# Decay attention and two gated MLPs in one kernel: a tile's attention cut into two halves of 64 tokens

## The chip, the cores and the metric

The kernel runs on one core of a Trainium2 chip. The metric is device time in microseconds (us), as the median of a few executions; a profile of one further execution gives the trace that the rows below are read from. TensorE does the matrix products (PE in the rows, its weight loads PEld), VectorE (DVE), ScalarE (ACT) and GpSimd (POOL) work element by element, and SyncE (SP) issues the transfers.

## What is computed

Inputs are `r, k, v` of 4 batches, 8 heads, 768 tokens and 48 dimensions, a decay `w` and a bonus `u`. The attention is a recurrence with one 48x48 state per head:

```python
for t in range(S):
    kt, vt, rt = (k[:, :, t], v[:, :, t], r[:, :, t])
    cur = np.einsum('bhd,bhe->bhde', u[None] * kt, vt)
    y[:, :, t] = np.einsum('bhd,bhde->bhe', rt, state + cur)
    state = w[None, :, :, None] * state + np.einsum('bhd,bhe->bhde', kt, vt)
```

Its output, 3072 tokens by 384, goes through two gated MLPs with 1536 hidden units. The first normalises its input and uses `g * sigmoid(g) * val`, the second `sigmoid(g) * val`; each multiplies by its output weights. Weights arrive in double precision, and a product in the MLPs is made of three single-pass products of high and low parts.

## The kernel before

**Tiles and blocks.** The tokens are 24 attention tiles of 128; tile i is chunk i // 4 of batch i % 4, so that a batch's state is needed again four tiles later. Four tiles make a block of 512 tokens, and there are six blocks. Each MLP layer handles a block in 12 steps, one for each 128 hidden units; a step is nine matmuls for the gate (lines 678 to 680), nine for the value, and nine or twelve for the output (line 705), all 512 or 384 columns long. Attention of later blocks is put between the steps of earlier ones. The first five tiles run before the first step.

**One tile's attention.** The decay is folded into `kq` and `rq` ahead of the products. Their transposes `kT` and `rT` hold a pair of heads in rows 0 to 47 and 64 to 111, so that the two heads of a pair lie in the two row halves of the array.
1. *Scores* (line 498): for each of four pairs and both heads, `kT` of 48x128 stays in the array and 128 columns of `rT` stream through, into one bank per head of the pair.
2. *Update* (line 502): `kq` transposed times `v` over all 128 tokens, eight products of 48x48, into a third bank. The last chunk of a batch has none.
3. VectorE multiplies the scores by a 128x128 triangular mask into `aa` (line 512), two instructions of 512 columns.
4. *Result*: the old state `z` enters with 32 products (line 525; none in the first chunk), each with 32 tokens as the array's columns; then `aa` times `v` with 32 products (line 530), over all 128 rows of the array and again with 32 tokens as columns.
5. VectorE adds the bonus term `vc` (line 536) and makes the new state `(z + update) * wc` (lines 545, 548 and 466), `wc` being the decay of a whole tile, which `state_factors` prepares at the start (line 417).

Each of these fp32 products shows in the trace as two MATMUL records.

**What sets the order.** `Plan` holds tasks with an engine, a price in us, a due time and the buffers that they read and write. `run` issues them in the order that its own clock finds, engine by engine, and hands out the eight PSUM banks. `DUE` gives the due time of a tile's attention against its block's first step, `LEAD` that of a weight piece's steps, `STEP` how far the elementwise part of an MLP step is preferred, and `S_US` and `Y_US` are the prices of the score task (scores and update) and of the result task. Each engine then works through its list strictly in order. Weights of the first layer come in as 36 pieces: a load, two ScalarE passes (lines 64 and 71), two VectorE ones (lines 80 and 81), a GpSimd sum (line 87), and high and low parts (lines 640 and 643).

Of the kernel before, what the change touches and what calls it, by code (L numbers as in the profile page):

```python
# [7 lines left out]
F32 = mybir.dt.float32  # L8
# [4 lines left out]
ALU = mybir.AluOpType  # L13
AX = mybir.AxisListType

P = 128
HS = 112
NPAIR = 4
# [6 lines left out]
DUE = (-75, 4), (-36, 5), (-41, 6)  # L25


LEAD = 17, 20, 18, 15, 14, 18
STEP = 12


Y_US, S_US = (1.4, 0.95), (1.6, 1.1)
# [198 lines left out]
def blocked(  # L231
# [31 lines left out]
    def ring(name, n, shape, dtype=F32):  # L263
        return [work.tile(shape, dtype, name=f"{name}{i}") for i in range(n)]
# [8 lines left out]
    mask = const.tile([P, P], F32, name="mask")  # L273
# [15 lines left out]
    x, z = ring("x", 2, [P, DM]), ring("z", B, [HS, NPAIR, D])  # L289
    xh, xl = ring("xh", 2, [P, KC, N], F32R), ring("xl", 2, [P, KC, N], F32R)  # L290
# [12 lines left out]

    half_of = lambda a, n: a.rearrange("p (q a) d -> p a q d", a=2)[:, n]
# [23 lines left out]
    def setup():  # L328
# [3 lines left out]
        def warm(banks):  # L332
            for bank in banks:
                nc.tensor.matmul(plan.banks[bank][:, :NPAIR * D], o[0][:, :P], o[0][:, :NPAIR * D], start=True, stop=True)
# [7 lines left out]
        for t in (kn[0], rn[0], kq[1], rq[0]):  # L342
# [11 lines left out]
        nc.gpsimd.affine_select(out=mask, in_=mask, compare_op=ALU.is_gt, fill=0.0,  # L354
                                base=0, pattern=[[1, P]], channel_multiplier=-1)
# [101 lines left out]
    def attention(i):  # L457
# [37 lines left out]
        def scores(*sp):  # L495
            for p in range(NPAIR):
                for n in range(2):
                    nc.tensor.matmul(sp[n][:, p * P:(p + 1) * P], kT[i2][rows(n), p, :], rT[i2][rows(n), p, :], start=True, stop=True)  # L498

        def update(up):  # L500
            for h in range(H):
                nc.tensor.matmul(up[rows(h % 2), h // 2 * D:(h // 2 + 1) * D], kq_[:, h, :], vn[i3][:, h, :], start=True, stop=True)  # L502

        def both(*ps):
            scores(*ps[:2])
            if not last:
                update(ps[2])
        more = [] if last else [name("up")]
        add("T", S_US[last], d + 3, both, [(t, i2, n) for t in ("kT", "rT") for n in range(2)] + ([] if last else [("kq", i2), ("v", i3)]),
            [name("sp")] + more, psum=[name(("sp", n)) for n in range(2)] + more, gate=[("aa", n) for n in range(2)])  # L510
        for n in range(2):
            add("V", 0.6, d + 3 + n, lambda sp, n=n: nc.vector.tensor_tensor(  # L512
                out=aa[0][:, n], in0=sp.rearrange("p (q t) -> p q t", q=NPAIR),
                in1=mask.unsqueeze(1).to_broadcast([P, NPAIR, P]), op=ALU.mult),
                [name("sp")], [("aa", n)], psum=[name(("sp", n))])
# [3 lines left out]
        quarters = [slice(t, t + P // 4) for t in range(0, P, P // 4)]  # L519
# [12 lines left out]
        banks = [name(("yp", n)) for n in range(2)]  # L532
        add("T", Y_US[first], d + 6, result, [("aa", 0), ("aa", 1), ("v", i3)] + ([] if first else [("rT", i2, 0), ("rT", i2, 1), ("z", b)]),
            [name("yp")], psum=banks, gate=[("x", i2)])
# [5 lines left out]


        if not last:
            u3 = lambda up: up[:HS, :NPAIR * D].rearrange("p (q e) -> p q e", q=NPAIR)
            if first:
                add("V", 0.27, d + 9, lambda up: nc.vector.tensor_tensor(out=z[b], in0=u3(up), in1=wc, op=ALU.mult),
                    [name("up"), "wc"], [("z", b)], psum=[name("up")])
            else:
                add("V", 0.27, d + 9, lambda up: nc.vector.tensor_tensor(out=z[b], in0=u3(up), in1=z[b], op=ALU.add),
                    [name("up")], [("z", b)], psum=[name("up")])
                add("VG", (0.27, 0.6), d + 9, either(z[b], z[b], wc, ALU.mult), ["wc"], [("z", b)])  # L550


        t = ss[i2]
# [212 lines left out]
    plan.add("V", 1.0, DUE[0][0] + 4, state_factors, (), ["wc", ("sg", 1)])  # L766
    plan.add("V", 0.3, DUE[0][0] + 16, start_ok, (), ["ok"])
# [189 lines left out]
```

## Time and profile before

| | us |
|---|---|
| median of three runs | 1038.29 (1037.9 to 1042.92) |
| the profiled execution | 1038.28 |
| its span, first to last instruction | 1036.6 |
| TensorE busy | 1013.8 (98%) |
| VectorE busy | 494.6 (48%) |
| ScalarE busy | 342.0 (33%) |
| GpSimd busy | 140.5 (14%) |

The profiled execution is as long as the median run, and 1.7 us of it lie outside its span. A matmul's recorded duration overlaps that of the next, since they are pipelined; what a matmul costs TensorE is the time from its start to the start of the next. Busy shares are averages over the whole span: the first 140 us, in which weights are prepared, look different from the rest.

### The profile page before, as it was taken

How to read it: one execution, taken by the hardware profiler on the slowest of the kernel's cores; microseconds unless marked ns; L12 is line 12 of the kernel's file. 1: busy time of each engine (PE TensorE's matmuls, PEld its weight loads, DVE VectorE, ACT ScalarE, POOL GpSimd, SP SyncE). 2: the span in 40 equal slices, each digit the busy share in tenths (PEclk: the TensorE clock that was granted, in tenths of full speed). 3: DMA queues.
4: the chain of work that ended last, by engine and by line, in shares of the span. 5: the costliest groups of instructions: out<-in, count | busy, mean ns of one | idle time of the engine just before them, and what ended most of it. 6: DMA issues, size and time to landing. Idle time of an engine off the chain costs nothing.

```text
span 1036.6 us, 18973 instructions
## 1 busy us (share of the span) xinstructions
PE 1013.8 (98%) x7746; PEld 841.5 (81%) x7746; DVE 494.6 (48%) x967; ACT 342.0 (33%) x710; POOL 140.5 (14%) x167
## 2 busy tenths in 40 slices
PE   7898999999999999999999999999999999999997
PEld 6686777787787777878888888888888888888886
DVE  8989975746654764563456322322222222222222
ACT  4676542223333333333455412222212212212121
POOL 4534342201212321111011000000000000000000
PEclk7999999999999999999999999999999999999999
DMA  9924446645783775553655200100100100000000
GB/s 191 265 88 123 116 84 134 113 92 138 155 199 85 166 177 127 135 147 116 183 157 175 73 1 1 61 1 1 61 1 20 42 1 1 31 1 21 11 1 34
DMA packets 213759, 91.37 MB, mean 88 GB/s; under 512 B 156576, under 2 KB 205984, under 8 KB 213664
## 3 DMA queue, kind: packets, MB, share of 16 engines
q1 hardware_dynamic: 213664, 90.08, 35.1%
q8 instruction: 62, 1.02, 0.4%
q14 instruction: 33, 0.27, 0.1%
HBM read 64.10 MB, written 25.95 MB: 87 GB/s over the span
## 4 chain that ended last, share of the span: by engine, by line
PE 90%; DVE 5%; DMA 2%; ACT 1%; SPq 1%; issue 1%; DVEq 0%; ACTq 0%
PE bank L705 28%; PE bank L678 19%; PE bank L679 19%; PE bank L680 19%; PE bank L498 2%; PE bank L530 2%; DMA wraw<-in_moe_w_val_dram 1%; PE bank L525 1%; DVE w L643 1%; DMA wraw<-in_moe_w_gate_dram 1%; PE bank L502 1%; DVE aa L512 1%; SPq L307 1%; DVE vc L466 1%; DVE wraw L81 1%
## 5 line engine op out<-in xcount | busy, mean ns | idle before, releaser
L678 PE MATMUL bank<-xh,w 128*128 128x512 f32 x864 | 344.8, 399 | 2.2 <-ACT w L640 1.6
L680 PE MATMUL bank<-xh,w 128*128 128x512 f32 x864 | 342.7, 397 | 1.3 <-DVE w L643 1.3
L679 PE MATMUL bank<-xl,w 128*128 128x512 f32 x864 | 342.8, 397 | 0.0
L687 DVE TENSOR_TENSOR sg<-bank,sg 128x512 f32<-128x512 f32 x144 | 99.4, 690 | 393.5 <-PE bank L680 391.5
L680 PEld LDWEIGHTS bank<-xh,w 128*128 128x128 f32 x864 | 162.9, 189 | 41.3 <-DVE w L643 2.9
L678 PEld LDWEIGHTS bank<-xh,w 128*128 128x128 f32 x864 | 162.8, 188 | 39.3 <-ACT w L640 2.1
L685 ACT ACTIVATE sg<-bank 128x512 f32<-128x512 f32 x144 | 86.0, 597 | 320.7 <-PE bank L680 320.6
L679 PEld LDWEIGHTS bank<-xl,w 128*128 128x128 f32 x864 | 162.9, 189 | 35.3 <-DVE xl L580 0.3
L689 ACT ACTIVATE hh<-sg 128x512 fp32r<-128x512 f32 x144 | 90.8, 631 | 233.3 <-DVE sg L687 233.3
L705 PE MATMUL bank<-w,hh 128*128 128x384 f32 x576 | 158.7, 337 | 0.0
L705 PE MATMUL bank<-hh,w 128*128 128x512 f32 x432 | 151.6, 402 | 0.1
L690 DVE TENSOR_TENSOR hl<-sg,hh 128x512 fp32r<-128x512 f32 x144 | 101.6, 706 | 64.3 <-ACT hh L689 64.1
L705 PEld LDWEIGHTS bank<-w,hh 128*128 128x128 f32 x576 | 105.0, 188 | 3.4
L705 PEld LDWEIGHTS bank<-hh,w 128*128 128x128 f32 x432 | 81.7, 189 | 20.4 <-DVE w L643 0.5
L705 PE MATMUL bank<-w,hl 128*128 128x384 f32 x288 | 96.7, 336 | 0.0
L705 PE MATMUL bank<-hl,w 128*128 128x512 f32 x216 | 85.9, 398 | 0.0
L705 PEld LDWEIGHTS bank<-w,hl 128*128 128x128 f32 x288 | 54.1, 188 | 3.3 <-DVE hl L690 0.3
L87 POOL TENSOR_TENSOR wt<-wraw 128x384 int32<-128x384 int32 x36 | 33.3, 926 | 172.2 <-DVE wraw L81 102.8
L66 ACT ACTIVATE wt<-wraw 128x384 f32<-128x384 f32 x72 | 39.6, 551 | 41.6 <-DMA wraw<-in_moe_w_gate_dram 24.8
L705 PEld LDWEIGHTS bank<-hl,w 128*128 128x128 f32 x216 | 40.9, 189 | 9.0
L87 POOL TENSOR_TENSOR wraw<-wraw 128x384 int32<-128x384 int32 x36 | 38.6, 1080 | 62.7 <-DVE wraw L81 42.7
L81 DVE SCALAR_TENSOR_TENSOR wraw<-wraw,wt 128x384 int32<-128x384 int32 x72 | 41.7, 587 | 1.4
(120 smaller groups left out, 706.6 us busy)
## 6 DMA issues: line engine op xcount, KB each, us to landing
wraw<-in_moe_w_gate_dram SPq DMA_DIRECT2D x24, 384.0 KB, 4.3
wraw<-in_moe_w_val_dram SPq DMA_DIRECT2D x24, 384.0 KB, 4.5
wraw<-in_moe_w_out_dram SPq DMA_DIRECT2D x24, 384.0 KB, 4.3
parked<-wt SPq DMA_DIRECT2D x36, 192.0 KB, 2.9
wt<-parked SPq DMA_DIRECT2D x36, 192.0 KB, 2.4
kn<-in_k_dram SPq DMA_DIRECT2D x24, 192.0 KB, 3.5
rn<-in_r_dram SPq DMA_DIRECT2D x24, 192.0 KB, 4.0
vn<-in_v_dram SPq DMA_DIRECT2D x24, 192.0 KB, 4.0
```

The source lines that it names most:

```text
L66: nc.scalar.activation(t.bitcast(F32), raw[:, :, 1].bitcast(F32), AF.Abs, scale=2.0 ** -112, accum_out=total)
L81: yield nc.vector.scalar_tensor_tensor(out=high, in0=high, scalar=-(1 << 31), in1=t, op0=ALU.bitwise_and, op1=ALU.bitwise_or)
L87: nc.gpsimd.tensor_tensor(out=out, in0=raw[:, :, 1], in1=raw[:, :, 0], op=ALU.add)
L498: nc.tensor.matmul(sp[n][:, p * P:(p + 1) * P], kT[i2][rows(n), p, :], rT[i2][rows(n), p, :], start=True, stop=True)
L678: nc.tensor.matmul(ps, whi[f][:, kind, ws], xh[b2][:, c, :], start=(c == 0), stop=False)
L679: nc.tensor.matmul(ps, whi[f][:, kind, ws], xl[b2][:, c, :], start=False, stop=False)
L680: nc.tensor.matmul(ps, wlo[f][:, kind, ws], xh[b2][:, c, :], start=False, stop=(c == KC - 1))
L685: add("A", 0.6, d - STEP, lambda g: nc.scalar.activation(sg[n2], g, gate), [("g", n)], [("sg", n2)], psum=[("g", n)])
L687: add("V", 0.69, d + 1 - STEP, lambda ps: nc.vector.tensor_tensor(out=sg[n2], in0=ps, in1=sg[n2], op=ALU.mult), [("value", n)], [("sg", n2 ...
L689: add("A", 0.63, d + 1 - STEP, lambda: nc.scalar.activation(hh[n2], sg[n2], AF.Copy), [("sg", n2)], [("hh", n2)])
L690: add("VG", (0.69, 1.5), d + 1 - STEP, lambda e: by[e].tensor_tensor(out=hl[n2], in0=sg[n2], in1=hh[n2].bitcast(F32), op=ALU.subtract), [( ...
L705: nc.tensor.matmul(a[:, :rhs.shape[-1]], lhsT, rhs, start=(f == 0 and i == 0), stop=(f == NF - 1 and i == 2))
```

## The change

The tile's 128 tokens are treated as two halves of 64. Scores are made within a half only: 16 products of 48x64 by 64 columns in place of eight of 48x128 by 128, so that the masked scores `aa` have 256 columns per head of a pair and the mask is 128x64. The update is made for each half apart (16 products over 64 tokens, eight in a batch's last chunk, which before had none), into the free columns of the two score banks, so that the third bank is gone. A new VectorE step `zh` adds the first half's update to the old state, and `zu` adds the second's; the new state is `zu * wc`. The result takes `z` for the first half of the tokens and `zh` for the second, with 16 products of 64 tokens each (eight in the first chunk, which before had none), then `aa` times `v` with 32 products over 64 rows and 32 tokens. Every product of 64 rows and up to 64 columns uses a quarter of the array, those of `aa` an eighth.

```diff
-DUE = (-75, 4), (-36, 5), (-41, 6)
-LEAD = 17, 20, 18, 15, 14, 18
-STEP = 12
-Y_US, S_US = (1.4, 0.95), (1.6, 1.1)
+DUE = (-74, 5), (-36, 5), (-40, 6)
+LEAD = 17, 21, 19, 16, 15, 19
+STEP = 13
+Y_US, S_US = (1.35, 1.15), (1.15, 1.0)
...
+    zh, zu = ring("zh", 2, [HS, NPAIR, D]), ring("zu", 2, [HS, NPAIR, D])
+    part = lambda n: slice(P // 2 * n, P // 2 * (n + 1))
+    state_of = lambda ps: ps[:, N // 2:N // 2 + NPAIR * D]
...
-        def scores(*sp):
+        def both(*sp):
+            for p in range(NPAIR):
+                for s in range(2):
+                    for n in range(2):
+                        nc.tensor.matmul(sp[n][part(s), p * P // 2:(p + 1) * P // 2], kT[i2][rows(n), p, part(s)],
+                                         rT[i2][rows(n), p, part(s)], start=True, stop=True)
             for p in range(NPAIR):
                 for n in range(2):
-                    nc.tensor.matmul(sp[n][:, p * P:(p + 1) * P], kT[i2][rows(n), p, :], rT[i2][rows(n), p, :], start=True, stop=True)
-        def update(up):
-            for h in range(H):
-                nc.tensor.matmul(up[rows(h % 2), h // 2 * D:(h // 2 + 1) * D], kq_[:, h, :], vn[i3][:, h, :], start=True, stop=True)
+                    for s in range(1 if last else 2):
+                        nc.tensor.matmul(state_of(sp[s])[rows(n), p * D:(p + 1) * D], kq_[part(s), 2 * p + n, :],
+                                         vn[i3][part(s), 2 * p + n, :], start=True, stop=True)
...
+        if first:
+            add("V", 0.27, d + 4, lambda sp: nc.vector.tensor_copy(zh[i2], u3(sp)), [name("sp")], [("zh", i2)], psum=banks[:1])
+        else:
+            add("V", 0.27, d + 4, lambda sp: nc.vector.tensor_tensor(out=zh[i2], in0=u3(sp), in1=z[b], op=ALU.add),
+                [name("sp"), ("z", b)], [("zh", i2)], psum=banks[:1])
+        if not last:
+            add("V", 0.27, d + 6, lambda sp: nc.vector.tensor_tensor(out=zu[i2], in0=u3(sp), in1=zh[i2], op=ALU.add),
+                [name("sp"), ("zh", i2)], [("zu", i2)], psum=banks[1:])
...
         def result(*yp):
-            for p in range(NPAIR if not first else 0):
-                for ts in quarters:
+            for p in range(NPAIR):
+                for s in range(1 if first else 0, 2):
                     for n in range(2):
-                        nc.tensor.matmul(yp[n][ts, p * D:(p + 1) * D], rT[i2][rows(n), p, ts], z[b][rows(n), p, :],
-                                         start=(p == 0), stop=False, skip_group_check=True)
-            for n in range(2):
-                for p in range(NPAIR):
-                    for ts in quarters:
-                        nc.tensor.matmul(yp[n][ts, p * D:(p + 1) * D], aa[0][:, n, p, ts], vn[i3][:, 2 * p + n, :],
-                                         start=(first and p == 0), stop=True, skip_group_check=True)
+                        nc.tensor.matmul(yp[n][part(s), p * D:(p + 1) * D], rT[i2][rows(n), p, part(s)],
+                                         (zh[i2] if s else z[b])[rows(n), p, :], start=(p == 0), stop=False, skip_group_check=True)
+            for p in range(NPAIR):
+                for n in range(2):
+                    for q in range(2):
+                        for s in range(2):
+                            ts = slice(P // 4 * q, P // 4 * (q + 1))
+                            nc.tensor.matmul(yp[n][part(s)][ts, p * D:(p + 1) * D], aa[0][part(s), n, p, ts], vn[i3][part(s), 2 * p + n, :],
+                                             start=(first and not s and p == 0), stop=True, skip_group_check=True)
...
-    plan.add("V", 1.0, DUE[0][0] + 4, state_factors, (), ["wc", ("sg", 1)])
+    plan.add("V", 0.9, DUE[0][0] + 24, state_factors, (), ["wc", ("sg", 1)], port=True)
```

The new prices and due times change the order of every engine. Three places matter.

TensorE, a tile of a middle chunk between MLP steps, before: an operand's name ends in a buffer number and a running one, `bank5_78` is PSUM bank 5, and the sizes are those of the output.

```order
L680 MATMUL bank6_79<-xh1_125,w11_1703 128x512
L498 MATMUL bank5_78<-rT0_115,kT0_113 128x128
L498 MATMUL bank4_77<-rT0_115,kT0_113 128x128
...
L502 MATMUL bank7_80<-vn0_99,kq0_102 48x48 x8
...
L525 MATMUL bank6_79<-z0_120,rT0_115 32x48
L525 MATMUL bank5_78<-z0_120,rT0_115 32x48
...
L530 MATMUL bank6_79<-vn0_99,aa0_117 32x48 x16
L530 MATMUL bank5_78<-vn0_99,aa0_117 32x48 x16
L678 MATMUL bank4_77<-xh0_124,w0_435 128x512
```

The same tile in the changed kernel:

```order
L714 MATMUL bank6_79<-hh0_134,w10_1647 128x512
L508 MATMUL bank7_80<-rT0_115,kT0_113 64x64
L508 MATMUL bank2_75<-rT0_115,kT0_113 64x64
...
L513 MATMUL bank7_80<-vn0_99,kq0_102 48x48
L513 MATMUL bank2_75<-vn0_99,kq0_102 48x48
...
L541 MATMUL bank4_77<-z0_120,rT0_115 64x48
L541 MATMUL bank7_80<-z0_120,rT0_115 64x48
L541 MATMUL bank4_77<-zh0_124,rT0_115 64x48
L541 MATMUL bank7_80<-zh0_124,rT0_115 64x48
...
L548 MATMUL bank4_77<-vn0_99,aa0_117 32x48 x4
L548 MATMUL bank7_80<-vn0_99,aa0_117 32x48 x4
...
L687 MATMUL bank2_75<-xh0_128,w1_922 128x512
```

The block of scores and update has 8 + 8 matmuls before and 16 + 16 now, the result 32 + 32 before and 16 + 32 now; both blocks stand between MLP matmuls as they did, and the update has no bank of its own any more.

VectorE, the steps between the two blocks of that tile, before:

```order
L512 TENSOR_TENSOR aa0_117<-bank5_78,mask_87 128x512
L512 TENSOR_TENSOR aa0_117<-bank4_77,mask_87 128x512
L690 TENSOR_TENSOR hl1_133<-sg1_129,hh1_131 128x512
L536 TENSOR_TENSOR x0_118<-bank6_79,vc0_105 128x4x48
L548 TENSOR_TENSOR z0_120<-bank7_80,z0_120 112x192
L536 TENSOR_TENSOR x0_118<-bank5_78,vc0_105 128x4x48
L466 TENSOR_TENSOR z0_120<-z0_120,wc_90 112x192
```

And in the changed kernel:

```order
L519 TENSOR_TENSOR aa0_117<-bank7_80,mask_87 128x4x64
L519 TENSOR_TENSOR aa0_117<-bank2_75,mask_87 128x4x64
L529 TENSOR_TENSOR zh0_124<-bank7_80,z0_120 112x192
L532 TENSOR_TENSOR zu0_126<-bank2_75,zh0_124 112x192
L696 TENSOR_TENSOR sg0_132<-bank5_78,sg0_132 128x512
L729 COPY o1_139<-bank1_74 128x512
L699 TENSOR_TENSOR hl0_136<-sg0_132,hh0_134 128x512
L554 TENSOR_TENSOR x0_118<-bank4_77,vc0_105 128x4x48
L474 TENSOR_TENSOR z0_120<-zu0_126,wc_90 112x192
L554 TENSOR_TENSOR x0_118<-bank7_80,vc0_105 128x4x48
```

Three VectorE steps, no longer two, stand between scores and result, two of them half as long; the state's sum has moved ahead of the result.

VectorE at the start, before, from `state_factors` (which writes `wc`) to the first weight piece:

```order
L417 COPY wc_90<-p2_83 112x192
L316 TENSOR_TENSOR wT_81<-wT_81,wsafe_82 112x4
L421 MEMSET ok_91 128x1
L422 TENSOR_REDUCE ok_91<-wT_81 112x1
L466 TENSOR_TENSOR kq1_103<-kn1_98,wk_88 128x8x48
...
L512 TENSOR_TENSOR aa0_117<-bank1_74,mask_87 128x512
L545 TENSOR_TENSOR z0_120<-bank2_75,wc_90 112x192
L80 TENSOR_SCALAR wt0_140<-wt0_140 128x384
L475 TENSOR_REDUCE cf1_108<-vc1_106 128x8
L81 SCALAR_TENSOR_TENSOR wraw0_308<-wraw0_308,wt0_140 128x384
```

In the changed kernel:

```order
L519 TENSOR_TENSOR aa0_117<-bank0_73,mask_87 128x4x64
L519 TENSOR_TENSOR aa0_117<-bank1_74,mask_87 128x4x64
L474 TENSOR_TENSOR vc0_105<-vn0_99,cf0_107 128x384
L527 COPY zh0_124<-bank0_73 112x192
L474 TENSOR_TENSOR vc1_106<-vc1_106,u_bc_84 128x384
L532 TENSOR_TENSOR zu0_126<-bank1_74,zh0_124 112x192
L483 TENSOR_REDUCE cf1_108<-vc1_106 128x8
L322 TENSOR_TENSOR sg1_133<-sg1_133 112x4 x3
L322 TENSOR_TENSOR p2_83<-sg1_133 112x4
L425 COPY wc_90<-p2_83 112x192
...
L80 TENSOR_SCALAR wt0_144<-wt0_144 128x384
```

`state_factors` now comes after the first tile's masks, and the first weight piece after the masks of the first four tiles, where it stood after those of the first.

## Rows read from the trace of the kernel before

**Rows 1.** The page: TensorE's busy time, and busy tenths in 40 slices.

```profile
PE 1013.8 (98%) x7746; PEld 841.5 (81%) x7746; DVE 494.6 (48%) x967; ACT 342.0 (33%) x710; POOL 140.5 (14%) x167
...
PE   7898999999999999999999999999999999999997
...
DVE  8989975746654764563456322322222222222222
```

**Rows 2.** Stretches: length, busy us (count) of PE, PEld, DVE, ACT, POOL; PEclk.

```profile
43.00:60.00 17.00, 17.00 (x67) 13.48 (x68) 13.19 (x28) 14.48 (x37) 7.25 (x8) 0.91 0.71 196
60.00:75.00 15.00, 15.00 (x66) 12.10 (x65) 14.37 (x26) 10.19 (x25) 6.25 (x6) 1.00 0.25 80
...
105.00:120.00 15.00, 14.61 (x212) 11.37 (x212) 14.74 (x32) 7.69 (x19) 7.93 (x5) 1.00 0.42 98
120.00:139.00 19.00, 17.37 (x214) 13.28 (x213) 16.84 (x39) 9.94 (x24) 6.40 (x9) 0.91 0.42 112
...
300.00:400.00 100.00, 100.00 (x1010) 79.95 (x1009) 58.65 (x119) 33.90 (x75) 24.46 (x27) 1.00 0.67 153
```

**Rows 3.** Chain that ended last, the first 150 us: start, us, what it was.

```profile
33.15 0.60 DVE aa L512
...
36.27 0.27 DVE x L536
...
39.35 2.13 issue
...
126.56 4.48 DMA wraw<-in_moe_w_val_dram
...
132.65 0.44 ACT w L640
...
136.19 3.09 PE bank L705 x9
...
148.01 2.10 PE bank L705 x9
```

**Rows 4.** Timeline of one middle-chunk tile, TensorE: start, us, line, operands, count.

```profile
229.20 1.16 PE L498 MATMUL bank<-rT,kT 48*128 48x128 f32 x16
...
230.29 0.56 PE L502 MATMUL bank<-vn,kq 128*48 128x48 f32 x16
...
230.79 0.50 PE L705 MATMUL bank<-hh,w 128*128 128x512 f32 x1
...
235.18 0.81 PE L525 MATMUL bank<-z,rT 48*32 48x48 f32 x64
...
235.92 0.89 PE L530 MATMUL bank<-vn,aa 128*32 128x48 f32 x64
...
236.74 0.50 PE L678 MATMUL bank<-xh,w 128*128 128x512 f32 x1
```

**Rows 5.** TensorE's attention groups from 139 to 470 us: records, busy us, mean ns.

```profile
L498 PE MATMUL bank<-rT,kT 48*128 48x128 f32 x256 | 18.6, 285 | 0.0
L530 PE MATMUL bank<-vn,aa 128*32 128x48 f32 x1024 | 14.2, 208 | 0.0
L525 PE MATMUL bank<-z,rT 48*32 48x48 f32 x1024 | 12.9, 211 | 0.0
L502 PE MATMUL bank<-vn,kq 128*48 128x48 f32 x192 | 6.8, 212 | 0.0
```

**Rows 6.** Timeline at the start: the warming matmuls of 192 columns (line 334).

```profile
6.41 0.82 PE L334 MATMUL bank<-o 128*128 128x192 f32 x4
7.06 0.60 PE L326 MATMUL bank<-ident,rn 128*112 128x128 f32 x4
```

**Rows 7.** Timeline of a tile with only nine matmuls between its two blocks.

```profile
460.76 0.50 PE L678 MATMUL bank<-xh,w 128*128 128x512 f32 x1
460.86 1.29 DVE L512 TENSOR_TENSOR aa<-bank,mask 128x512 f32<-128x512 f32 x2 [1.39 <-PE bank L498]
...
463.06 0.81 PE L525 MATMUL bank<-z,rT 48*32 48x48 f32 x64
```

More of the change, by code (lines that the diff above doesn't have):

```diff
@@ L272, in blocked @@
     ident = const.tile([P, P], F32, name="ident")
-    mask = const.tile([P, P], F32, name="mask")
+    mask = const.tile([P, P // 2], F32, name="mask")
     wk = const.tile([P, H, PAD], F32, name="wk")
@@ L333, in warm @@
             for bank in banks:
-                nc.tensor.matmul(plan.banks[bank][:, :NPAIR * D], o[0][:, :P], o[0][:, :NPAIR * D], start=True, stop=True)
+                nc.tensor.matmul(state_of(plan.banks[bank]), o[0][:, :P], o[0][:, :NPAIR * D], start=True, stop=True)
         def turn_raw(bank, t):
@@ L353, in setup @@
         nc.gpsimd.memset(mask, 1.0)
-        nc.gpsimd.affine_select(out=mask, in_=mask, compare_op=ALU.is_gt, fill=0.0,
-                                base=0, pattern=[[1, P]], channel_multiplier=-1)
+        for part, base in ((mask, P // 2), (mask[:P // 2], 0)):
+            nc.gpsimd.affine_select(out=part, in_=part, compare_op=ALU.is_gt, fill=0.0,
+                                    base=base, pattern=[[1, P // 2]], channel_multiplier=-1)
         nc.gpsimd.memset(one, 1.0)
@@ L500, in update @@
-        def update(up):
-            for h in range(H):
-                nc.tensor.matmul(up[rows(h % 2), h // 2 * D:(h // 2 + 1) * D], kq_[:, h, :], vn[i3][:, h, :], start=True, stop=True)
[L504 to L510, printed above, removed]
@@ L511, in attention @@
-        for n in range(2):
[L512 to L519, printed above, removed]
+                    for s in range(1 if last else 2):
+                        nc.tensor.matmul(state_of(sp[s])[rows(n), p * D:(p + 1) * D], kq_[part(s), 2 * p + n, :],
+                                         vn[i3][part(s), 2 * p + n, :], start=True, stop=True)
@@ new lines, in attention @@
+        banks = [name(("sp", n)) for n in range(2)]
+        add("T", S_US[last], d + 3, both, [(t, i2, n) for t in ("kT", "rT") for n in range(2)] + [("kq", i2), ("v", i3)],
+            [name("sp")], psum=banks, gate=[("aa", n) for n in range(2)] + [("zh", i2)])
+        for n in range(2):
+            add("V", 0.33, d + 3 + n, lambda sp, n=n: nc.vector.tensor_tensor(
+                out=aa[0][:, n, :, :P // 2], in0=sp[:, :N // 2].rearrange("p (q t) -> p q t", q=NPAIR),
+                in1=mask.unsqueeze(1).to_broadcast([P, NPAIR, P // 2]), op=ALU.mult),
+                [name("sp")], [("aa", n)], psum=[banks[n]])
@@ new lines, in attention @@
+        u3 = lambda sp: state_of(sp)[:HS].rearrange("p (q e) -> p q e", q=NPAIR)
+        if first:
[6 more added lines that the diff above has]
+                [name("sp"), ("zh", i2)], [("zu", i2)], psum=banks[1:])
@@ L532, in attention @@
+            for p in range(NPAIR):
[5 more added lines that the diff above has]
+                                             start=(first and not s and p == 0), stop=True, skip_group_check=True)
         banks = [name(("yp", n)) for n in range(2)]
-        add("T", Y_US[first], d + 6, result, [("aa", 0), ("aa", 1), ("v", i3)] + ([] if first else [("rT", i2, 0), ("rT", i2, 1), ("z", b)]),
-            [name("yp")], psum=banks, gate=[("x", i2)])
+        add("T", Y_US[first], d + 6, result, [("aa", 0), ("aa", 1), ("v", i3), ("rT", i2, 0), ("rT", i2, 1), ("zh", i2)]
+            + ([] if first else [("z", b)]), [name("yp")], psum=banks, gate=[("x", i2)])
@@ L542, in attention @@
         if not last:
[L543 to L550, printed above, removed]
+            add("VG", (0.27, 0.6), d + 10, either(z[b], zu[i2], wc, ALU.mult), ["wc", ("zu", i2)], [("z", b)])
         t = ss[i2]
@@ L765, in blocked @@
     parks = 0.0
-    plan.add("V", 1.0, DUE[0][0] + 4, state_factors, (), ["wc", ("sg", 1)])
-    plan.add("V", 0.3, DUE[0][0] + 16, start_ok, (), ["ok"])
+    plan.add("V", 0.9, DUE[0][0] + 24, state_factors, (), ["wc", ("sg", 1)], port=True)
+    plan.add("V", 0.3, DUE[0][0] + 30, start_ok, (), ["ok"], port=True)
     attend(0)
```

## The prediction, made before the changed kernel ran

> **What bounds the kernel now.** I read the page first, then the stretches, then the chain, then single tiles. The page has TensorE busy for 98% of the span, and VectorE at 8 or 9 tenths only in the first slices [rows 1]. The stretches split the span in two. From 43 to 139 us VectorE is the full engine: 14.37 us of 15, later 14.74 of 15, and 16.84 of 19, while TensorE has gaps [rows 2]; the chain there is made of weight loads, the passes over them and VectorE steps, ending with a load at 126.56 and the high part made of it at 132.65 [rows 3]. After 139 us TensorE has no gap: 100.00 us of 100.00, at the full one of the clock's two levels (PEclk 1.00, 2.4 GHz), with VectorE at 58.65 [rows 2]. So after 139 us each microsecond of TensorE work that goes shortens the run by a microsecond, and before it VectorE's work and the supply of weights count.
>
> After 139 us there are 256 score records at 16 a tile, hence 16 tiles, of which 192/16 = 12 have an update and four, the last chunk's, have none; all 16 have both parts of the result (1024 records each, 64 a tile) [rows 5].
>
> **What a tile costs TensorE before.** From start to start [rows 4]: scores 229.20 to 230.29, 1.09 us for 16 records, 68 ns each; update to 230.79, 0.50 us, 31 ns each; the state's part 235.18 to 235.92, 0.74 us for 64 records, 11.6 ns each; `aa` times `v` to 236.74, 0.82 us, 12.8 ns each. Sum 3.15 us; in a last chunk, without update, 2.65 us.
>
> **A price for a quarter of the array.** No row shows a 64x64 quarter, so I build one. Streaming: four records of 192 columns take 7.06 - 6.41 = 0.65 us, 163 ns each or 0.85 ns a column [rows 6]; that makes 41 ns for 48 columns, 54 for 64 and 109 for 128. Scores stand in two places of the array (the row halves), so a place is taken for 2 x 68 = 136 ns a record, 27 more than streaming; the update in two column halves, 2 x 31 = 62, 21 more; `aa` in four column strips, 4 x 12.8 = 51, 10 more. The surplus goes with the stationary columns: 10 for 32, 21 for 48, 27 for 128. For 64 I take 23. Do row and column cuts work together? The state's part uses both, two row halves by four strips, and is denser than `aa` with strips alone (11.6 against 12.8 ns) although its records stream as many columns, so they do at least in part. I take all four quarters as working at once.
>
> - Scores: 32 records of 64 columns, (54 + 23)/4 = 19.3 ns, 0.62 us (before 1.09).
> - Update: 32 records, 62/4 = 15.5 ns, 0.50 us (before 0.50). In the last chunk 16 records in two quarters, 31 ns, 0.50 us (before none).
> - State: 32 records of 48 columns with 64 stationary, (41 + 23)/4 = 16 ns, 0.51 us (before 0.74).
> - `aa` times `v`: 64 records in four column strips as before, each over 64 rows rather than 128; 0.82 us as before.
>
> Sum 2.45 us for either kind, which saves 0.70 us in 12 tiles and 0.20 us in four: 8.4 + 0.8 = **9.2 us**, all of it in the stretch where TensorE is full.
>
> Bounds. Below: every record at the densest row, 11.6 ns, and scores at streaming alone, 54/4 = 13.6 ns, gives 0.43 + 0.37 + 0.37 + 0.74 = 1.91 us, and 1.87 in a last chunk (its update 16 x 41/2 ns = 0.33): 12 x 1.24 + 4 x 0.78 = 18 us saved. Above: only two quarters at work at a time gives 1.23 + 0.99 + 1.02 + 0.82 = 4.06 us, and 3.57 in a last chunk: 0.91 us lost in each of 16 tiles, 14.6 us. I stay by 2.45 because the update's and `aa`'s own rows, with their streams unchanged, carry half of it.
>
> **The bank rule.** In the state's part, whose row halves write two different banks [rows 4], nothing waits. The new `aa` products put consecutive matmuls of the two row halves into different partitions of one bank, and no row of before does that. The Trainium skill ("TensorEngine Tiling (Array Packing)", Restrictions and Gotchas, Gotcha 1) says that row tiles cannot access one PSUM bank at the same time and that software has to see to it; no run here shows it yet. Were such matmuls kept apart, a record would hold the array for at least its 41 ns of streaming: 64 x 41 ns = 2.6 us for 0.82. That is a rival below.
>
> **The new wait.** The result now needs `zh` as well as `aa`, and behind the result stand all further MLP matmuls of TensorE's list. From VectorE's slots in the chain, 512 columns take 0.60 us and 192 take 0.27 [rows 3], hence 0.34 for 256. Before, two masks: 1.20 us. Now 0.34 + 0.34 + 0.27 = 0.95 us. The shortest distance between the blocks is nine MLP matmuls in both orders, 460.76 to 463.06, with the masks starting at 460.86 [rows 7]: 2.2 us for 0.95, so nothing waits, even if a 0.7 us step of the MLP slips in between. If it did wait, each 0.1 us would cost 16 x 0.1 = 1.6 us. The state's product with `wc` is wanted four tiles later and costs nothing. VectorE's other changes after 139 us lie in its 40% of idle time.
>
> **The first 139 us.** Eight tiles lie there. VectorE: 16 masks at 0.34 for 0.60 save 4.2 us; `zh` and `zu` for the old sum add 8 x 0.27 = 2.2; the first four tiles also get a product with `wc`, 1.1 at most, less where GpSimd takes it. About 1 us less of VectorE's work in 139. TensorE's saving there goes into its gaps. `state_factors` only moves later. The first weight piece is handled after the masks of four tiles, not of one, but the first MLP step has to wait for the fourth tile's normalised output anyway, and VectorE's steps up to that come to about the same sum in both orders. I take 0.6 us of the 1 us as gained. What I can't cost from rows is the new order of loads: a single missed load shows as a gap of some 2 us and then a stretch at the lower level (1.2 GHz). The nine matmuls at 136.19 took 3.09 us, those at 148.01 2.10 [rows 3], and PEclk 0.91 over 19 us [rows 2] is 1.7 us lost. So one such event is worth about 3.8 us, either way.
>
> **Sum.** 1038.28 (the profiled execution, equal to the median within 0.01) - 9.2 - 0.6 = **1028.5 us**.
>
> **The rivals.**
> - *The start gets longer.* One or two more gaps with their slow stretch: 1032 to 1036. For it: VectorE is full there, the order of loads is new, the chain had a 2.13 us pause for issuing at 39.35 [rows 3], and the first four tiles have 24 matmuls more each. Against: VectorE has slightly less to do. It decides against a clear gain from 4.6 us of added start.
> - *The start gets shorter.* The gap before 133 us and its slow stretch go: 1024 to 1025. For it: VectorE's steps queue ahead of that last load, and there are fewer of them. Against: the weights themselves are as many.
> - *Quarters cost less than a column's surplus says.* Loads hide behind streaming, down to the lower bound: 1020 to 1024. For it: the state's part at 11.6 ns, where eight places share. Against: `aa`, with four places, pays its 10 ns.
> - *Row halves do not work at once* (slower; the change then doesn't do what it says). With two quarters at a time 1038.3 + 14.6 - 0.6 = 1052; with the quarters as forecast but `aa` kept apart by its bank, 1028.5 + 16 x 1.8 = 1057. It turns the result once a middle tile costs more than 3.15 us, that is, when `aa` takes over 1.5 us, 24 ns a record. Against it: the state's part works in row halves and strips together. For it: no row has two row halves in one bank.
>
> **How the numbers follow.** Forecast 0.60, own range 1024.5 to 1032; longer start 0.16; shorter start 0.08; cheaper quarters 0.10; no overlap 0.06. A range from 1021 to 1036 leaves out the last, a part of the cheap quarters and the worst starts, some 0.13. A measurement of this kernel can tell about 0.5% from no change, that is 5.2 us: faster means under 1033.1, which is the forecast, the two gains and a quarter of the longer starts, 0.82; within 0.5%, 0.12; slower 0.06.
>
> **What would show it.** In a tile's timeline after 139 us: scores start to start near 0.62 us, update 0.50, state 0.51, `aa` 0.82; the first MLP matmul of the second block's stretch without gaps again at about 139 us; VectorE's 256-column mask near 0.41 us long, 0.34 in slots; no TensorE gap ahead of the result. Wrong would be an `aa` group well over 0.82 us, a score group near 1.1 us, gaps ahead of line 541, or a gapless stretch that starts some microseconds earlier or later.

## The result and the profile after

The changed kernel takes **1029.88 us** (median of 6 runs, 1026.99 to 1032.21) against 1038.46 for the kernel before (6 runs, 1037.9 to 1042.92): a ratio of 0.9907, with a 95% interval of 0.9882 to 0.9933. It is faster, by 8.6 us; the prediction was 1028.5. The profiled execution of the changed kernel took 1029.34 us, its span 1027.7.

The page of the changed kernel, busy times and then tenths of TensorE and VectorE in 40 slices, beside [rows 1]:

```profile
PE 1002.4 (98%) x7938; PEld 831.1 (81%) x7938; DVE 490.4 (48%) x993; ACT 341.7 (33%) x710; POOL 140.2 (14%) x170
...
PE   7799999999999999999999999999999999999997
...
DVE  7889995645655664653555322222222223222222
```

TensorE has 192 records more and 11.4 us less to do. Its share stays at 98%, and the picture in slices is the same: a start in which VectorE is full, then TensorE alone.

The stretches of the changed kernel, with the columns of [rows 2]:

```profile
43.00:60.00 17.00, 16.28 (x124) 12.27 (x119) 14.19 (x26) 11.01 (x29) 7.08 (x7) 0.81 0.60 191
...
120.00:139.00 19.00, 18.23 (x230) 13.78 (x228) 18.45 (x42) 12.72 (x32) 9.83 (x11) 1.00 0.52 126
139.00:460.00 321.00, 320.61 (x3678) 255.53 (x3679) 195.17 (x418) 101.31 (x219) 69.98 (x79) 1.00 0.64 142
460.00:1020.00 560.00, 560.00 (x2623) 480.08 (x2621) 169.70 (x270) 157.25 (x280) 10.70 (x12) 1.00 0.13 43
```

After 139 us TensorE idles for 0.39 us in 881. Before that the start has another shape: the granted clock is lower between 43 and 60 us (0.81, before 0.91), and the lower stretch between 120 and 139 us is gone (1.00, before 0.91).

One middle tile of the changed kernel on TensorE, as [rows 4] shows it before (start, us, line, operands, count):

```profile
228.62 0.69 PE L508 MATMUL bank<-rT,kT 48*64 48x64 f32 x32
229.13 0.54 PE L513 MATMUL bank<-vn,kq 64*48 64x48 f32 x32
229.60 0.50 PE L687 MATMUL bank<-xh,w 128*128 128x512 f32 x1
...
236.09 0.26 PE L541 MATMUL bank<-z,rT 48*64 48x48 f32 x2
236.10 0.26 PE L541 MATMUL bank<-zh,rT 48*64 48x48 f32 x2
236.18 0.23 PE L541 MATMUL bank<-z,rT 48*64 48x48 f32 x2
236.19 0.23 PE L541 MATMUL bank<-zh,rT 48*64 48x48 f32 x2
236.24 0.23 PE L541 MATMUL bank<-z,rT 48*64 48x48 f32 x2
...
236.70 0.89 PE L548 MATMUL bank<-vn,aa 64*32 64x48 f32 x64
237.51 0.50 PE L687 MATMUL bank<-xh,w 128*128 128x512 f32 x1
```

From start to start, median of the 16 tiles:

| us | scores | update | state | `aa` times `v` | tile |
|---|---|---|---|---|---|
| before | 1.09 | 0.50 | 0.74 | 0.82 | 3.14 |
| predicted | 0.62 | 0.50 | 0.51 | 0.82 | 2.45 |
| after | 0.515 | 0.47 | 0.61 | 0.81 | 2.41 |

A last chunk's tile went from 2.64 to 2.40 us.

**Where the time went.** The two orders of work pass a common point: 320 MLP matmuls have started (221 of gate and value, 99 of output) and eight tiles are done. Before, the 321st starts there at 142.71 us and the last one of the run 885.85 us later; after, at 142.92 us, and 876.90 us later. The start thus lost 0.2 us and the rest gained 8.95. In the rest the MLP matmuls, each from its start to the next start, take 837.49 us in both traces, and the attention blocks of the 16 tiles take 48.25 us before and 39.29 after (two other matmuls take the remaining 0.12). That difference, 8.96 us, is the whole gain.

### The profile page after: what moved, and what is told of

It reads as the page before. It is cut to its first block, busy times and chain, and to the rows that moved or that the text cites. A ratio compares the mean times of both kernels' runs of the same rounds, so it can differ in the third digit from the quotient of the medians.

```text
span 1027.7 us, 19397 instructions
## 1 busy us (share of the span) xinstructions
PE 1002.4 (98%) x7938; PEld 831.1 (81%) x7938; DVE 490.4 (48%) x993; ACT 341.7 (33%) x710; POOL 140.2 (14%) x170
## 4 chain that ended last, share of the span: by engine, by line
PE 87%; DVE 8%; DMA 1%; ACT 1%; issue 1%; POOL 0%; SPq 0%; DVEq 0%; POOLq 0%; ACTq 0%
PE bank L714 27%; PE bank L687 18%; PE bank L688 18%; PE bank L689 18%; PE bank L548 2%; DVE wraw L81 1%; PE bank L541 1%; PE bank L508 1%; DVE w L652 1%; DVE wt L80 1%; DVE hl L699 1%; DMA rn<-in_r_dram 1%; PE bank L513 1%; DVE vc L474 1%; DVE sg L696 0%
```

## Experiments

The kernels are measured at the same common point (the table gives the profiled execution). "Rest" is the time from there to the start of the last MLP matmul. The kernel before took between 1038.35 and 1039.05 us (median) on the chips that these ran on. A kernel with one run has no interval. A common point belongs to one execution: the four kernels that have the changed tables and differ from the changed kernel at most in the order of the score or `aa` products (after, q2, q3, q4) pass it between 141.04 and 145.10 us, so a difference at the start is good to a few microseconds only, while the rests of the kernels with the same attention repeat to 0.3 us.

| kernel | us, median (runs) | ratio, 95% interval | common point | rest |
|---|---|---|---|---|
| before | 1038.46 (6) | | 142.71 | 885.85 |
| after | 1029.88 (6) | 0.9907, 0.9882 to 0.9933 | 142.92 | 876.90 |
| t1_tables_only | 1036.97 (8) | 0.9974, 0.9958 to 0.9990 | 142.27 | 885.92 |
| t2_old_tables | 1033.55 (4) | 0.9951, 0.9934 to 0.9967 | 147.68 | 876.91 |
| s1_old_due | 1029.10 (4) | 0.9911, 0.9889 to 0.9934 | 143.53 | 876.66 |
| s2_old_lead | 1033.23 (10) | 0.9947, 0.9928 to 0.9967 | 147.96 | 876.66 |
| q1_quartered_only | 1040.85 (10) | 1.0025, 1.0015 to 1.0035 | 143.97 | 886.75 |
| q2_one_quarter | 1040.18 (1) | | 141.04 | 888.91 |
| q3_two_quarters | 1033.26 (1) | | 142.31 | 880.83 |
| q4_banks_apart | 1031.03 (1) | | 145.10 | 876.79 |
| r1_state_last | 1029.71 (4) | 0.9910, 0.9887 to 0.9933 | 143.90 | 876.60 |
| m4_four_first | 1030.58 (4) | 0.9919, 0.9888 to 0.9949 | 144.20 | 877.31 |
| r2_joined | 1029.36 (4) | 0.9912, 0.9892 to 0.9932 | 144.88 | 875.28 |

### The tables alone, and the attention alone

t1_tables_only is the kernel before with the new numbers and places:

```diff
-DUE = (-75, 4), (-36, 5), (-41, 6)
-LEAD = 17, 20, 18, 15, 14, 18
-STEP = 12
+DUE = (-74, 5), (-36, 5), (-40, 6)
+LEAD = 17, 21, 19, 16, 15, 19
+STEP = 13
-    plan.add("V", 1.0, DUE[0][0] + 4, state_factors, (), ["wc", ("sg", 1)])
+    plan.add("V", 0.9, DUE[0][0] + 24, state_factors, (), ["wc", ("sg", 1)], port=True)
```

(`start_ok` moves likewise.) t2_old_tables is the changed kernel with the reverse of this diff.

> The kernel before, with the due times, leads, step and the places of state_factors and start_ok of the changed kernel, its attention as it was. Theory (the gain is TensorE work taken out of the 16 tiles after 139 us): no gain, 1036 to 1041 us, and the stretch from TensorE's last gap to the end stays near 897 us. Rival (the gain comes from the new order): under 1033 us.

> The changed kernel with the due times, leads, step and places of the kernel before. Theory: the gain stays, 1027 to 1033 us, and the gapless stretch is near 888 us. Rival (the new order brings it): 1036 us or more.

Both came out as the theory had it, t2 half a microsecond above its range. The rests fall into two classes: 885.9 us with the old attention, 876.9 with the new, whichever tables go with it. So the gain after 139 us belongs to the attention alone. The start does not split that way. The old attention passes the common point at 142.71 us with old tables and at 142.27 with new ones; the new attention at 147.68 with old tables and at 142.92 with new ones. In these executions the new attention by itself makes the start 5.0 us longer, and the new tables take that back. By the medians of the runs it is some 4 us: t2 is 5.1 us faster than the kernel before on its chip (1038.65), where its rest alone is worth 8.9. Of the 5.0 us, 4.4 are already there at the first MLP matmul (47.36 us, before 42.99); what makes those first tiles longer is not shown. With the old attention the new tables alone are worth little: t1 is 1.7 us faster than the kernel before on that chip, with the same rest.

### Which number of the tables

s1_old_due is the changed kernel with the old `DUE` alone, s2_old_lead with the old `LEAD` and `STEP` alone:

```diff
-LEAD = 17, 21, 19, 16, 15, 19
-STEP = 13
+LEAD = 17, 20, 18, 15, 14, 18
+STEP = 12
```

> The changed kernel with the attention's due times of the kernel before (first tiles 4 apart, not 5) and everything else new, the leads of the weight pieces, the step and the place of state_factors among it. With all tables old the new attention took 1033.6 us, 144.1 us to the 306th MLP matmul. Theory 1 (the spacing of the first tiles costs the start): about 1033 us. Theory 2 (the weight pieces' leads do): about 1030 us.

> The changed kernel with the weight pieces' leads and the step of the kernel before and the new due times. Theory 1 (spacing): about 1030 us. Theory 2 (leads): about 1033 us. Either way the time from the 306th MLP matmul to the end stays near 881 us.

With the old due times the run is as fast as the changed kernel; with the old leads the common point comes at 147.96 us and the run is 3 to 4 us longer. So it is not the spacing of the tiles but `LEAD` and `STEP`, which were not run apart. `LEAD` is the distance at which a weight piece's load and its ScalarE, VectorE and GpSimd steps are due ahead of the step that needs them; all but the load's own entry, and `STEP`, are one larger in the changed kernel. The stretches from 75 to 105 and from 105 to 139 us (columns of [rows 2]) of the changed kernel:

```profile
75.00:105.00 30.00, 28.93 (x279) 22.58 (x278) 29.43 (x60) 20.89 (x54) 13.88 (x13) 1.00 0.60 152
105.00:139.00 34.00, 32.18 (x438) 24.50 (x436) 33.02 (x73) 20.90 (x51) 13.66 (x16) 1.00 0.47 112
```

and of s2_old_lead:

```profile
75.00:105.00 30.00, 28.61 (x274) 21.22 (x274) 27.54 (x56) 19.09 (x49) 13.52 (x13) 1.00 0.54 152
105.00:139.00 34.00, 29.97 (x427) 22.50 (x426) 31.98 (x75) 21.43 (x53) 11.31 (x13) 1.00 0.41 100
```

VectorE, the engine that is full there, is busy for 62.45 of 64 us with the new leads and for 59.52 with the old ones, and less is moved by DMA (112 against 100 GB/s in the second stretch). VectorE has less to do per tile, and with the old leads it then waits where it could work on weights. One wait makes up 2.2 of these 2.9 us. It stands in VectorE's waits of s2_old_lead from 75 to 105 us (sum, times, longest) and is explained by its chain (start, us, what):

```profile
DVE wt L80 <- ACT wt L66: 2.2, 1, 2.2
...
94.56 0.48 DVE w L652
95.05 5.92 DMA wraw<-in_moe_w_gate_dram
100.99 0.65 ACT wt L66 x2
```

The chain goes from VectorE's last step on one piece (line 652, the low part, read from `wraw`) to the load of another piece, which lands 5.92 us later, and from there to ScalarE's pass on it, for which VectorE waits. The larger leads make such last steps due earlier. In the changed kernel no wait of VectorE in the two stretches is over 0.4 us. That the rest of the 5 us is lost in the same way is not shown.

### Is it the quarters, or the columns?

q1_quartered_only is the kernel before with its full scores, all 128 tokens by 128, made in quarters: 16 products of 64 stationary columns with 128 streamed, in place of eight of 128 with 128.

```diff
-                for n in range(2):
-                    nc.tensor.matmul(sp[n][:, p * P:(p + 1) * P], kT[i2][rows(n), p, :], rT[i2][rows(n), p, :], start=True, stop=True)
+                for s in range(2):
+                    for n in range(2):
+                        hs = slice(P // 2 * s, P // 2 * (s + 1))
+                        nc.tensor.matmul(sp[n][hs, p * P:(p + 1) * P], kT[i2][rows(n), p, hs], rT[i2][rows(n), p, :], start=True, stop=True)
```

> The kernel before with its full scores made in quarters of the array: 16 products of 48x64 by 128 columns for eight of 48x128, nothing left out, the same result. Theory (halving the columns saves; the quarters only keep the array full): 8 rounds of four records, each as long as 128 columns, about 112 ns, as now; score block 1.0 to 1.1 us, run 1037 to 1040 us. Rival (small tiles are denser by themselves, as the 16 ns a record of the changed kernel suggest): 32 x 16 ns to 32 x 20 ns, 0.5 to 0.65 us, run near 1031 us.

A tile of it on TensorE:

```profile
230.35 1.10 PE L500 MATMUL bank<-rT,kT 48*64 48x128 f32 x32
231.38 0.56 PE L504 MATMUL bank<-vn,kq 128*48 128x48 f32 x16
```

The scores take 1.03 us, where they took 1.09. Cutting the array into quarters gains almost nothing as long as each product streams as many columns; the scores outside the two halves, which the change no longer makes, are what was saved. The run even got 0.25% slower, a little above the range expected. Its start is 1.3 us longer and its rest 0.9: what the scores gain (16 times 0.06 us) is lost again in two score blocks, at 356 and 371 us, which take 0.25 and 0.66 us more because they stop until a transfer into `rT` has landed, and TensorE stops for 0.6 us among MLP matmuls at 362 us, where the profile shows nothing that it waited for.

### Do the four quarters work at once?

The changed kernel with the score products in another order. In q2_one_quarter four products in a row use the same quarter, in q3_two_quarters consecutive ones share a column half:

```diff
 # q2_one_quarter
-            for p in range(NPAIR):
-                for s in range(2):
-                    for n in range(2):
+            for s in range(2):
+                for n in range(2):
+                    for p in range(NPAIR):
 # q3_two_quarters
-            for p in range(NPAIR):
-                for s in range(2):
+            for s in range(2):
+                for p in range(NPAIR):
```

> The changed kernel with the order of the score products changed so that four in a row use the same quarter of the array. Theory (four quarters work at once, and a record holds its quarter some 59 ns): 32 x 59 ns, about 1.9 us for the score block in place of 0.52, and 16 x 1.4 = 22 us more, 1052 us. Rival (fewer columns are enough, whatever the order): 0.52 us and 1030 us.

> The changed kernel with its score products ordered by token half first, so that only two quarters alternate. From the run with one quarter in a row (1.18 us for the block, not 1.9: TensorE started records of the next quarter ahead of the waiting ones) the theory is now: records of different quarters overlap as far as TensorE looks ahead, and the order decides how many. Two quarters alternating: 16 rounds of 59 ns at worst, 0.98 us, and with look-ahead between 0.6 and 0.98 us. Rival (order without effect): 0.52 us.

The same tile in q2_one_quarter:

```profile
230.10 1.36 PE L508 MATMUL bank<-rT,kT 48*64 48x64 f32 x29
231.25 0.25 PE L513 MATMUL bank<-vn,kq 64*48 64x48 f32 x3
231.30 0.22 PE L508 MATMUL bank<-rT,kT 48*64 48x64 f32 x1
...
231.44 0.55 PE L513 MATMUL bank<-vn,kq 64*48 64x48 f32 x23
```

and in q3_two_quarters:

```profile
229.15 0.80 PE L508 MATMUL bank<-rT,kT 48*64 48x64 f32 x26
229.74 0.25 PE L513 MATMUL bank<-vn,kq 64*48 64x48 f32 x2
...
229.93 0.55 PE L513 MATMUL bank<-vn,kq 64*48 64x48 f32 x26
```

The block of scores and update takes 1.83 us in q2 and 1.27 in q3, against 0.98 in the changed kernel, and the rest follows to a tenth: the attention blocks sum to 51.30 and 43.19 us, 12.01 and 3.90 more than after, and the rests are 12.01 and 3.93 longer. So the quarters do work at once when the order lets them, and the order is worth up to 12 us of this kernel. But q2 came out at about 1.2 us of scores, where the theory, 32 records one after another, had 1.9. The rows show why: update records (line 513) start at 231.25, ahead of score records (line 508) that come before them in the program and start at 231.30 and later. TensorE started a record whose quarter was free ahead of earlier ones that waited for theirs. The changed kernel does the same: the two records of a product stand next to each other in the program (at 364 us, below, a block stops behind the first product's two), but its scores start in rounds of four, one record to each quarter.

### The bank rule

q4_banks_apart lets consecutive row halves of `aa` write two banks, where the changed kernel has them write one:

```diff
-                for n in range(2):
+                for m in range(2):
                     for q in range(2):
                         for s in range(2):
+                            n = m ^ s
```

> The changed kernel with the products of aa ordered so that consecutive matmuls of the two row halves write different banks; same products, same rotation of the four places. Theory (two row halves in one bank, on different partitions, do not disturb each other): the aa block stays at 0.81 us. Rival (the rule on row tiles and banks costs something): it gets shorter than 0.81 us.

Its `aa` group, from start to start, is 0.814 us in the median of 16 tiles, exactly that of the changed kernel, and its rest, 876.79 us, is the same within 0.1. Two row halves writing different partitions of one bank cost nothing here. This single run is 1.2 us longer than the changed kernel's median, and the difference lies ahead of the common point, which it passes at 145.10 us.

### Taking the new wait away

r1_state_last makes the products of `aa` first and those of `z` and `zh` behind them, so that the result waits for `zh` half a microsecond or more later:

```diff
-                for s in range(1 if first else 0, 2):
-                    for n in range(2):
-                        nc.tensor.matmul(yp[n][part(s), ...], rT[i2][rows(n), p, part(s)], (zh[i2] if s else z[b])[rows(n), p, :], start=(p == 0), stop=False, ...)
-            for p in range(NPAIR):
...
+            for p in range(NPAIR):
+                for s in range(1 if first else 0, 2):
+                    for n in range(2):
+                        nc.tensor.matmul(yp[n][part(s), ...], rT[i2][rows(n), p, part(s)], (zh[i2] if s else z[b])[rows(n), p, :], start=False, stop=True, ...)
```

> The changed kernel with the result's two parts exchanged: aa times v first, then the state's part, so that the wait for zh stands behind 32 products. Theory (the 0.15 us ahead of the aa block is a drain between tile shapes, and moves): state and aa together stay at 1.43 us after 139 us; the waits for zh, 2.6 us at the start and one of 0.3 us later, go. If the start's wait for zh is what made the first MLP step late (46.1 us for 43.0), the run falls by 1 to 3 us to some 1028 us; if VectorE's work and the weights set the start, it stays at 1030 us.

What the result of the changed kernel waits for (two rows of line 541 in TensorE's waits: sum in us, times, longest):

```profile
PE bank L541 <- DVE zh L527: 2.6, 2, 1.4
...
PE bank L541 <- DVE zh L529: 0.8, 1, 0.8
```

and that of r1_state_last:

```profile
PE bank L543 <- issue: 2.9, 2, 2.3
...
PE bank L543 <- DVE aa L519: 1.4, 2, 0.9
```

All of line 527's waits lie in the start (that line is the first chunk's). They are real, and without them nothing is won: the waits for `zh` are gone, waits for `aa` and idle time that the profile puts down to issue stand in their place, and the run takes 1029.71 us for 1029.88. After 139 us it is no different: where the changed kernel's state group once waits 0.31 us for `zh` (at 280 us, below), the `aa` group of r1_state_last waits 0.29 us for `aa`. Its rest is 0.3 us shorter (876.60 for 876.90) for another reason: the score block that stops for a transfer (364 us, below) takes 0.59 us in it and 0.86 in the changed kernel.

### Two tries at more

m4_four_first is r1_state_last with four tiles instead of five ahead of the first MLP step, r2_joined is r1_state_last with the result of a tile due just ahead of the next tile's scores, so that a change of the array's shape falls away:

```diff
 # m4_four_first
-DUE = (-74, 5), (-36, 5), (-40, 6)
+DUE = (-74, 5), (-33, 4), (-40, 6)
 # r2_joined
-        add("T", Y_US[first], d + 6, result, ...)
+        add("T", Y_US[first], due[i + 1] + 2.99 if 8 <= i < NTILE - 1 and (i + 1) % 4 else d + 6, result, ...)
```

> As r1_state_last, with the second block's attention due later (first entry -33, spacing 4 in place of -36 and 5), so that four tiles, not five, stand ahead of the first MLP step on TensorE. Theory (VectorE's sum of work sets the end of the start, the order on TensorE does not): the first MLP step comes some 3 us earlier, near 42 us, but the gapless stretch begins near 139 us as before, and the run stays within 2 us of r1_state_last. Rival (TensorE's order sets it): the whole 3 us are gained, 1026 us or less.

> As r1_state_last, with the result of tiles 8 to 22 due just ahead of the next tile's scores, so that a result (ending with 64x64 products) is followed at once by scores (64x64 too) without MLP matmuls between. In the list three of the twelve pairs come together, the others do not for want of inputs. Theory (each change between MLP matmuls and attention costs TensorE about 0.2 us on the way back and 0.1 us of drain on the way out): 0.3 us less for each joined pair, 1 us in all, 880 us from the 306th MLP matmul to the end, and the run not to be told from 1029.7 us. Rival (the late results come in too late for the next layer's block): gaps ahead of a block's first step, over 1031 us.

m4 moved the first MLP matmul only from 46.3 to 45.5 us, where some 3 us and a start near 42 us had been expected, and nothing of it was left at the common point. In r2 three of twelve pairs came to stand next to each other, one of them here:

```profile
243.51 0.23 PE L548 MATMUL bank<-zh,rT 48*64 48x48 f32 x2
243.56 0.66 PE L508 MATMUL bank<-rT,kT 48*64 48x64 f32 x32
244.04 0.54 PE L513 MATMUL bank<-vn,kq 64*48 64x48 f32 x32
```

Its rest is 1.3 us shorter than r1's. By the starts half of that comes from the three joined pairs, 0.2 us each where 0.3 had been expected (a result that is followed by scores costs 0.04 us at its end for 0.15 ahead of an MLP matmul, and the scores save 0.1 at their beginning); the other half is mostly short waits that r1 has and r2 has not. Its start is 1.0 us longer. Neither can be told from the changed kernel in time, so no version measured here beats it.

## Why the prediction held, step by step

- **What bounds the kernel, and so where the gain lies: right.** After 139 us a microsecond of TensorE's attention work was a microsecond of the rest, in the changed kernel and in q2 and q3 alike. The shares could not have told: TensorE is at 98% before and after. One reading ahead of 139 us was off: [rows 2] show TensorE without a gap from 43 to 75 us (17.00 of 17, 15.00 of 15) and VectorE at 13.19 of 17 in the first of these; TensorE's gaps begin only behind 75 us.
- **The tile's price: 2.41 us for 2.45, from two errors that cancel.** By the terms, twelve tiles at 3.14 - 2.41 = 0.73 us and four at 0.24 make 9.7 us, where the text had 9.2. The mis-sized terms are the scores, 0.10 us too dear (0.62 for 0.515), and the state, 0.10 too cheap (0.51 for 0.61). Both come from the step "a price for a quarter", streaming plus a surplus for the stationary columns. Most of that surplus was the end of a group: [rows 4] time a group to the start of the next one, and what passes behind its last record (0.20 us after the scores, some 0.14 after the others) was spread over all its records. Without these ends a score record of the kernel before takes its place for 112 ns, an update record for 45 and an `aa` record for 43, only 2 to 4 ns above the streaming of the text, which read 27, 21 and 10. In the changed kernel a quarter with 64 stationary columns is taken for 58 ns a record, whether 64 columns stream through it (scores) or 48 (state, 236.18 to 236.24 above), and one with 48 of either for 45 ns. The larger of the two counts; they don't add. So the scores don't have the 23 ns of surplus, and in the state's group the 64 stationary columns govern, not the 48 streamed; another 0.15 us pass behind its last record, where the array changes its shape for `aa`.
- **Four quarters at once: right,** though it was argued from the state's part alone. q2 and q3 show it for the scores. That it takes records started out of order was not in the text.
- **The bank rule.** The prediction gave it 0.06 as a rival, with `aa` at 2.6 us. It measures 0.81 us, with one bank or two (q4). The rule of the Trainium skill ("TensorEngine Tiling (Array Packing)", Restrictions and Gotchas, Gotcha 1), that row tiles cannot access one PSUM bank at the same time, had no price in this kernel; the measurement decides for this pattern, in which the two row halves also write different partitions of the bank.
- **"Nothing waits" for `zh`: nearly.** The mask is 413 ns long on average in the first 140 us and 0.34 in slots (279.42 to 280.09 below for two), as forecast, and the 2.2 us of [rows 7] did cover the new steps. Two short waits were not forecast. At 280 us VectorE had taken a 1.38 us step, for a later tile's bonus term, ahead of the masks, although the scores had been done by 278 us (columns: start, us, what, and in brackets the idle time before it):

```profile
278.11 1.38 DVE L474 TENSOR_TENSOR vc<-rn,kn 128x384 f32<-128x384 f32 x1 [3.17 <-DMA turn_x<-vc]
...
279.42 0.74 DVE L519 TENSOR_TENSOR aa<-bank,mask 128x256 f32<-128x256 f32 x2
...
280.09 0.34 DVE L529 TENSOR_TENSOR zh<-bank,z 112x192 f32<-112x192 f32 x1
280.15 0.32 PE L541 MATMUL bank<-z,rT 48*64 48x48 f32 x4
280.48 0.26 PE L541 MATMUL bank<-zh,rT 48*64 48x48 f32 x2
```

  `zh` ends at 280.43, the products with it start at 280.48, and the state's group takes 0.93 us instead of 0.61. The text allowed for a step of 0.7 us in between; this one was twice as long. At 364 us a score block took 0.86 us instead of 0.515. After the two weight loads of its first product it stopped until the second half of `rT` was there: that transfer, issued at 359.92 us, took 4.4 us, so it landed at 364.3 us (first the line of the transfers, with the starts of the two, then their times to landing, then the weight loads, where the profile calls the idle time "issue"):

```profile
L462 SPq DMA_DIRECT2D rT<-turn_r x2: 486/531/576, 358.8 to 359.9; - x2
...
DMA to landing us min/median/max: 3.6/4.0/4.4
...
363.98 0.19 PEld L508 LDWEIGHTS bank<-rT,kT 48*64 48x64 f32 x2 [0.36 <-issue]
...
364.40 0.52 PEld L508 LDWEIGHTS bank<-rT,kT 48*64 48x64 f32 x27 [0.23 <-issue]
```

  With a few smaller ones these waits cost 39.29 - (12 x 2.41 + 4 x 2.40) = 0.8 us of the 9.7.
- **The start: the right sum for half of the reason.** The text took 0.6 us as gained, from VectorE's shorter list, and called a longer start a rival with 0.16. The profiled execution lost 0.2 us. The first MLP matmul starts at 46.11 us, 3.1 us later than the 42.99 of before, and ahead of 139 us the low clock [rows 2] is gone and TensorE idles for 0.8 us in 19 instead of 1.6, which gives it back: the 281st MLP matmul still starts 2.4 us later than before, the 301st 0.2 us earlier. So each of the two rivals on the start came true in part, at about the sizes that were given, and that they cancel is luck as far as the text goes. What the step missed is that it treated the change as one thing: the attention alone costs the start 4 to 5 us (t2, s2), which VectorE's shorter list does not show, and the new leads and `STEP` are the part of the diff that pays for it. The same reasoning with the old tables would have given 1028.5 too, and been 5 us off (t2 took 1033.55).

In sum, the profiled execution: 1038.28 - 9.7 (work) + 0.8 (waits) + 0.2 (start) = 1029.6, and 0.2 us less behind the start of the last MLP matmul gives the 1029.34 that was measured.

## What to carry to other kernels

Find the stretch in which one engine has no gap, count the instructions there, and price them from start to start; the rest of the program can be bounded instead of summed. In a packed array write consecutive products so that they go to different places, and price a place by the larger of its stationary and its streamed columns; leaving out columns saves, cutting the array alone does not. Where a change comes with new scheduling numbers, run it once with the old numbers: the two may be hiding a cost from each other, and only the separate runs show it.

## What the runs showed of the hardware

- The time for which a place of the array was taken by one record went with the larger of stationary and streamed columns: 58 ns for 64 with 64 and for 64 with 48, 45 ns for 48 with 48, 43 ns for 32 with 48, 109 to 112 ns where 128 columns stream through 64 or 128. Records to different places start about 7 ns apart. This prices groups that keep two or four places in turn; the state's part of the kernel before, with eight places, took 11.6 ns a record where 43 ns in eight places would give 5.4.
- Where the next group uses the array in another shape, some 0.14 us stand at the end of a group: 0.148 us from state to `aa`, 0.133 to 0.138 from `aa` or the update to an MLP matmul. Between scores and update, both in quarters now, it is 0.04 us, and from a result to scores in r2, quarters too, the same; before, from scores in halves by rows to the update in halves by columns, it was 0.2 us. That is a part of why the scores' group shrank by more than half.
- TensorE started records out of the program's order where an earlier one waited for its quarter (q2, above). The Trainium skill ("TensorE: Matmul & The Clock Gate", The mechanism) says that matmuls start and end strictly in order; these starts differ. The changed kernel shows it in every tile: at 280 us, where `zh` is late, both records of the first `z` products start ahead of `zh` (four records at 280.15), while in an undisturbed tile the `zh` records at 236.10 start ahead of the second `z` records at 236.18. So its rounds of four are made by starts out of order, and without them, with each record behind the one before it in its quarter, the scores would presumably be dearer; no run here takes them away.
